# A fused chunk attention and two-layer network on one core: the last two blocks' first layer by 7 products, copies of q shared with GpSimd

## The chip, the cores and the metric

The kernel runs on one core of one Trainium2 chip. A core has a matrix engine, TensorE (PE in the profile, its weight loads PEld), and VectorE (DVE), ScalarE (ACT), GpSimd (POOL) and SyncE (SP), which run in parallel, each through its own list of instructions in order; they wait for each other by semaphores. DMA queues move data between the chip's memory, the on-chip SBUF and back; PE writes its sums to PSUM, from which ACT and DVE read. The metric is the device time of one launch in microseconds (us); lower is better.

## The reference

```python
scores = scale * np.matmul(q_c, k_c.transpose(0, 1, 2, 4, 3))   # chunks of 64 of 576 rows
scores = scores - np.max(scores, axis=-1, keepdims=True)
attn = np.exp(scores)
attn = attn / (np.sum(attn, axis=-1, keepdims=True) + 1e-09)
out = np.matmul(attn, v_c)
...
x = np.ascontiguousarray(attn_out.transpose(0, 2, 1, 3)).reshape(B * S, H * D)
...
h = x @ w_in                       # 4608 x 512 by 512 x 2048
g = np.maximum(0.01 * h, h)
return (g @ w_out).astype(np.float32)   # by 2048 x 512
```

q, k and v are float32 of shape 8 x 8 x 576 x 64: batch, heads, rows, head dimension. Attention stays within chunks of 64 rows. Its output, 4608 tokens by 512, goes through two layers with a leaky ReLU between.

## The kernel before

**Attention** works on 36 tiles of 128 tokens (u, two chunks each, all 8 heads). For a tile, q and k are loaded into a buffer `qk_in` (`NIN` = 9 of them) by DMAs that POOL issues, and turned: for tiles 0 to 9 by PE, from tile 10 by a transposing DMA that SP issues, into a buffer `QKT` (`NKT` = 6). Two copies, one for each half of the partitions, spread q into a zero-padded tile `QZ` (`spread_q`, L506; three tiles in turn). PE multiplies (`Sp`), DVE takes the maximum and subtracts it (`mx`, `sh`), ACT exponentiates (`ex`), DVE sums (`z`), POOL adds the 1e-9 (`ze`), DVE inverts (`zi`), POOL normalises (`en`; DVE for tiles below 9). The result is turned (`et`), PE multiplies by V (`xp`, from two buffers `VB` that hold one batch each, loaded by POOL's DMAs), and ACT stores the tile into `xT`, a ring of 12 tiles.

**The layers** work on 13 blocks of tokens: four of 128, two of 256, seven of 512. Blocks from 4 on do the second layer as a 2 x 2 block product by 7 products instead of 8 (Strassen's scheme): DVE forms four sums of quarters (`form`, L820: `S` and a reused part of `gT`), PE does products 1 to 7 (`product`, L842), each summing into one of three PSUM banks a, b, c, ACT copies intermediate states of bank b to SBUF (`td`, `tu`, `tw`), and DVE adds these to what the other banks hold (`osb`). Bank b carries products 1, 6, 7, 4 one after another, so each must wait until the sum so far has been copied.

**The first layer** of a block is 16 columns of 128 features. Done plainly (`mm1`, L748) a column takes 4 matmuls of 512 tokens (or the same work in two halves of 256, which `SUBS` sets), and ACT applies the ReLU (`gT<-hT`). In blocks 7 to 12 some of it is also done by 7 products: a pair k takes the columns 2k, 2k+1, 8+2k, 9+2k, which are 4 plain columns, and does them as 7 products of 4 matmuls with 256 columns each (`product1`, L953; rows `la`, `lb`, `lc`, named after the bank). `L1S` says which pairs of a block go this way; k = 0 to 3 would be all of it. The products need sums of quarters of x (`xf`, DVE, per block) and of w_in (`wq`, DVE, once per pair). In the trace, a pair's chain on bank b is: product 1, ACT's copy `ld`, product 6, copy `lu`, product 7, copy `lw`, product 4; DVE adds `ld`, `lw` and `lu` to the banks of products 2, 5 and 3; ACT then applies the ReLU to four results. The buffers of `ld`, `lu`, `lw` hold one pair (`temp1`, L970), so a pair's copies wait until the pair ahead of it is done with them; in the last two blocks `ld` has two buffers.

**The order** of every engine is set when the program is built, by a planner (`Planner`): it knows each task's duration from a table in the code, its dependencies and a position (`pos`), and at each step gives an engine the ready task with the lowest position. Positions of attention tasks follow from how far a tile runs ahead of its block (`LEAD`) and from tables of small corrections (`TWEAK`, `NUDGE`, `HOLD`); `LOADS` is the order of the first loads by hand (`g8`: q and k of tile 8; `v1.0`, `v1.1`: the halves of V of batch 1). The hardware runs each engine's list in that order, whatever the real durations are. Where PE has nothing in the first 24 us, filler matmuls (`idle`, L1183) are put.

The lines that set what runs where:

```python
L1S = {7: (0, 1), 8: (0, 1), 9: (0, 2), 10: (0, 1, 2), 11: (1, 2), 12: (0, 1, 2)}
COPY_P = ("ACT",)
ORDER1 = (1, 2, 6, 5, 7, 4, 3)
```

Of the kernel before, what the change touches and what calls it, by code (L numbers as in the profile page):

```python
# [164 lines left out]
def kernel(  # L165
# [31 lines left out]
    SUBS = {11: 512, 12: 512, 10: 512}  # L197
# [11 lines left out]
    ATT = -0.39  # L209
    FORM = -0.93  # L210
    WFAT = -2.31
# [5 lines left out]
    NORM_P = ()  # L217
    EXP8 = ()
    HOLD = {('v', 3): 28.7, ('k', 2): 14.1, ('q', 5, 0): 31.9, ('G', 0, 2, 0): 23.3, ('n', 0): 11.9, ('k', 3): 18.8, ('c', 0): 15.1, ('e', 0): 13.3, ('s', 2): 15.0, ('G', 2, 2, 0): 33.8, ('q', 5, 1): 29.5, ('m', 1): 11.9, ('G', 2, 3, 0): 32.8, ('tq', 0): 6.1, ('tk', 5): 30.8, ('G', 2, 0, 0): 28.6, ('m', 4): 29.4, ('tq', 2): 13.8, ('G', 1, 0, 0): 23.2, ('z', 3): 26.9, ('k', 4): 27.2, ('q', 2, 0): 14.8, ('m', 0): 9.0, ('s', 1): 12.0, ('G', 0, 1, 0): 25.4, ('x', 3): 25.7}
    NUDGE = {('M', 11, 7, 1): -0.03, ('M', 9, 1, 0): 0.01, ('xf', 7, 3): -0.05, ('cm', 10, 2): -0.08, ('L', 12, 1, 2): 0.15, ('form', 7, 3): -0.25, ('A', 11, 15, 0): 0.2, ('L', 12, 0, 1): -0.02}  # L220
    GUARD = 0.84
    DEPTH = 4
    DEEP = 40
    LATE = {'q': 0, 'c': 0, 's': 0.19}
    SPREAD = 1.01
# [4 lines left out]
    MARGIN = 2.08  # L230
    TWEAK = {(0, 4): -0.39, (5, 4): -0.05, (32, 1): 0.26, (4, 11): -0.13, (4, 2): 0.05, (0, 9): 0.13, (2, 2): 1.1, (1, 8): 0.02, (1, 6): 0.3, (9, 7): -0.15, (0, 5): -0.67, (4, 3): 0.2, (26, 9): 0.23, (20, 0): -0.51, (0, 10): -0.12}
    A_LEAD = 0.25
# [354 lines left out]
    def total(u):  # L587
        def emit(eng, tag, at):
            st["z", u] = sbp.tile([128, 8], FP32, name="z", tag="z", bufs=2)
            nc.vector.tensor_reduce(out=st["z", u], in_=st["ex", u], axis=AXL.X, op=ALU.add)  # L590
        return emit
# [83 lines left out]
    for u in range(NU):  # L675
# [35 lines left out]
        if u in ZE:  # L711
            add(("zr", u), dve, total(u), [("x", u)] + prev, pos=p(u, 8))
# [4 lines left out]
        ne = {"DVE": (0.70, 0.74), "POOL": (1.43, 1.48)}  # L717
# [116 lines left out]

    SF_FORMS = (5, 6, 7, 3)
# [4 lines left out]
    ADDED = {2: "d", 5: "w", 3: "u"}  # L840

    def product(j, m, p):  # L842
        def emit(eng, tag, at):
            g, n = gT(j), half_tokens(j)
            bank = BANKS[m]
# [5 lines left out]
            opens = m in OPENS  # L851
# [27 lines left out]
    def finish(j, m, step, p=None):  # L879


        def emit(eng, tag, at):
            ix = slice(None) if p is None else p
            of = BANK[j, BANKS[m]] if p is None else BANK[j, BANKS[m], p]
# [4 lines left out]
            if step == 0:  # L889
                either(eng, to, of)  # L890
            else:
                two = j in TWO2 and m != 3
                by = (BANK[j, "b"] if p is None else BANK[j, "b", p]) if two else temp(ADDED[m], j)[:, ix]
                nc.vector.tensor_tensor(out=to, in0=of, in1=by, op=ALU.add)
# [19 lines left out]
    WQ_: dict[tuple, bass.AP] = {}  # L914
    LB: dict[tuple, bass.AP] = {}
# [13 lines left out]
    def w_form(k, m):  # L929
        def emit(eng, tag, at):  # L930
# [6 lines left out]
            WQ_[k, m] = sbp.tile([128, 2, 256], FP16, name="wq", tag="wq", bufs=4 * len(early))  # L937
# [279 lines left out]
```

## Time and profile before

| | |
|---|---|
| median of 3 runs | 278.14 us (277.4 to 278.62) |
| the profiled execution, its own time | 278.49 us |
| its span, first to last instruction | 276.7 us |
| granted TensorE clock | 1.00 |

The page gives the busy time of each engine over the span. Times of instructions count from the span's start. A row of a timeline has the start, the length of the merged piece, engine, line, operation, what is written and read, and the count; in brackets stands the idle time of the engine just before it and what ended it. Matmuls overlap: a row's length holds the draining of its last matmul, so what a matmul costs PE is the distance from its start to the next one's. The lines that matter are shown where the prediction uses them.

### The profile page before, as it was taken

How to read it: one execution, taken by the hardware profiler on the slowest of the kernel's cores; microseconds unless marked ns; L12 is line 12 of the kernel's file. 1: busy time of each engine (PE TensorE's matmuls, PEld its weight loads, DVE VectorE, ACT ScalarE, POOL GpSimd, SP SyncE). 2: the span in 40 equal slices, each digit the busy share in tenths (PEclk: the TensorE clock that was granted, in tenths of full speed). 3: DMA queues.
4: the chain of work that ended last, by engine and by line, in shares of the span. 5: the costliest groups of instructions: out<-in, count | busy, mean ns of one | idle time of the engine just before them, and what ended most of it. 6: DMA issues, size and time to landing. Idle time of an engine off the chain costs nothing.

```text
span 276.7 us, 7303 instructions
## 1 busy us (share of the span) xinstructions
PE 268.9 (97%) x2992; PEld 231.8 (84%) x2992; DVE 200.0 (72%) x345; ACT 207.3 (75%) x380; POOL 135.4 (49%) x170
## 2 busy tenths in 40 slices
PE   7899999999999999999999999999999999999995
PEld 6789974689999999899999989997887787788884
DVE  7698867886694498679786976797769773854651
ACT  5447764687869898998879889977999478767611
POOL 8857653467774978377576844585220330000000
PEclk9999999999999999999999999999999999999999
DMA  8999999999999999999999999999956103200133
GB/s 141 155 184 161 184 194 155 214 135 182 130 197 165 158 163 191 118 83 145 232 138 152 182 209 165 121 112 242 127 97 172 21 19 97 76 2 0 39 134 133
DMA packets 161152, 38.21 MB, mean 138 GB/s; under 512 B 152160, under 2 KB 156768, under 8 KB 161120
## 3 DMA queue, kind: packets, MB, share of 16 engines
q0 software_dynamic: 114336, 18.09, 97.3%
q1 hardware_dynamic: 45744, 19.41, 38.6%
q8 instruction: 23, 0.38, 0.6%
q10 hardware_dynamic: 1040, 0.26, 0.4%
q14 instruction: 9, 0.07, 0.1%
HBM read 36.70 MB, written 9.44 MB: 167 GB/s over the span
## 4 chain that ended last, share of the span: by engine, by line
PE 82%; DMA 12%; POOL 4%; issue 1%; DVE 0%; POOLq 0%
PE hT L757 23%; PE mb L858 20%; PE mc L858 10%; PE lb L964 9%; PE ma L858 5%; PE lc L964 4%; DMA qk_in<-in_q_dram 4%; DMA w_outT<-in_moe_w_out_dram 4%; DMA qk_in<-in_k_dram 4%; PE xp L648 3%; PE Sp L540 2%; PE la L964 2%; POOL qk_in L327 2%; PE oP L780 2%; POOL w_inT L344 1%; POOL VB L335 1%
## 5 line engine op out<-in xcount | busy, mean ns | idle before, releaser
L757 PE MATMUL hT<-xT,w_inT 128*128 128x256 f16 (+2 forms) x768 | 88.3, 264 | 0.5 <-DMA w_inT<-in_moe_w_in_dram 0.2
L757 PEld LDWEIGHTS <-w_inT 128*128 128x128 f16 x768 | 63.6, 98 | 10.4 <-issue 0.9
L769 ACT ACTIVATE gT<-hT 128x512 f16<-128x512 f32 x88 | 50.6, 593 | 17.0 <-PE hT L757 16.7
L858 PEld LDWEIGHTS <-gT 128*128 128x128 f16 x512 | 49.4, 98 | 6.4
L596 POOL TENSOR_SCALAR ze<-z 128x8 f32<-128x8 f32 x31 | 10.5, 337 | 61.2 <-DVE z L590 60.8
L858 PEld LDWEIGHTS <-S 128*128 128x128 f16 x384 | 36.7, 98 | 4.3
L614 POOL TENSOR_TENSOR en<-ex,zi 128x512 f16<-128x512 f16 x27 | 31.1, 1151 | 15.3 <-ACT xT L658 3.8
L327 POOL DMA_DIRECT2D qk_in<-in_q_dram x39 | 34.1, 875 | 6.2 <-DMA w_outT<-in_moe_w_out_dram 2.6
L327 POOL DMA_DIRECT2D qk_in<-in_k_dram x39 | 34.1, 875 | 4.1 <-DMA w_outT<-in_moe_w_out_dram 1.3
L590 DVE TENSOR_REDUCE z<-ex 128x8 f32<-128x512 f16 x36 | 24.6, 682 | 12.2 <-ACT ex L584 11.8
L549 DVE TENSOR_REDUCE mx<-Sp 128x8 f32<-128x512 f32 x36 | 24.6, 682 | 11.8 <-PE Sp L540 11.6
L858 PE MATMUL mb<-WF,gT 128*128 128x256 f16 x256 | 33.0, 273 | 0.0
L858 PE MATMUL mc<-w_outT,S 128*128 128x256 f16 x256 | 33.0, 273 | 0.0
L276 ACT ACTIVATE QZ<-QKT 64x512 f16<-64x512 f16 x52 | 32.4, 624 | 0.6
L555 DVE TENSOR_TENSOR sh<-Sp,mx 128x512 f32<-128x512 f32 x36 | 24.7, 686 | 0.5
L964 PEld LDWEIGHTS <-wq 128*128 128x128 f16 x224 | 21.5, 98 | 3.3
L658 ACT ACTIVATE xT<-xp 128x512 f16<-128x512 f32 x36 | 21.3, 593 | 3.8 <-PE xp L648 3.6
L584 ACT ACTIVATE ex<-sh 128x512 f16<-128x512 f32 x36 | 22.6, 628 | 1.2 <-DVE sh L555 0.8
L335 POOL DMA_DIRECT2D VB<-in_v_dram x16 | 18.8, 1178 | 3.7 <-DMA w_outT<-in_moe_w_out_dram 1.8
L964 PEld LDWEIGHTS <-w_inT 128*128 128x128 f16 x168 | 16.0, 98 | 2.4
L858 PE MATMUL mb<-WF,S 128*128 128x256 f16 x128 | 16.6, 273 | 0.0
L858 PE MATMUL ma<-w_outT,gT 128*128 128x256 f16 x128 | 16.6, 273 | 0.0
(81 smaller groups left out, 445.1 us busy)
## 6 DMA issues: line engine op xcount, KB each, us to landing
out_dram<-osb SPq DMA_DIRECT2D x12, 512.0 KB, 4.7
VB<-in_v_dram POOLq DMA_DIRECT2D x16, 288.0 KB, 8.0
qk_in<-in_q_dram POOLq DMA_DIRECT2D x31, 128.0 KB, 7.0
qk_in<-in_k_dram POOLq DMA_DIRECT2D x31, 128.0 KB, 7.2
out_dram<-osb SPq DMA_DIRECT2D x10, 256.0 KB, 5.3
w_inT<-in_moe_w_in_dram POOLq DMA_DIRECT2D x8, 256.0 KB, 7.4
w_outT<-in_moe_w_out_dram POOLq DMA_DIRECT2D x4, 512.0 KB, 11.4
qk_in<-in_q_dram POOLq DMA_DIRECT2D x8, 64.0 KB, 7.7
```

The costliest lines, as they stand in the source:

```text
L276: nc.scalar.activation(out=out, in_=in_, func=AFT.Copy, bias=0.0, scale=1.0)
L327: nc.gpsimd.dma_start(out=qk[name, u][a - u * G:z - u * G], in_=SRC[name][a // S, :, a % S:a % S + z - a, :].rearrange("h p d -> p h d"),)
L335: nc.gpsimd.dma_start(out=VB[b % NVB][m * CH:(m + 1) * CH, :, c0:c1, m * CH:(m + 1) * CH], in_=v[b, m * H // 2:(m + 1) * H // 2, c0 * CH:c ...
L549: nc.vector.tensor_reduce(out=st["mx", u], in_=st["S", u], axis=AXL.X, op=ALU.max)
L555: nc.vector.tensor_tensor(out=st["sh", u], in0=st["S", u], in1=st["mx", u].unsqueeze(2).to_broadcast((128, 8, CH)), op=ALU.subtract,)
L584: nc.scalar.activation(out=st["ex", u], in_=st["sh", u], func=AFT.Exp, bias=0.0, scale=SCL)
L590: nc.vector.tensor_reduce(out=st["z", u], in_=st["ex", u], axis=AXL.X, op=ALU.add)
L614: (nc.vector if eng == "DVE" else nc.gpsimd).tensor_tensor(out=st["en", u], in0=st["ex", u], in1=st["zi", u].unsqueeze(2).to_broadcast((12 ...
L757: nc.tensor.matmul(out=hT[:, i, :], lhsT=w_inT[:, t, fc * 128:(fc + 1) * 128], rhs=xT[:, r0 % RING // G:(r0 % RING + tb) // G, t, :], star ...
L769: nc.scalar.activation(out=gT(j)[:, nf * a:nf * a + nf, h * tb:h * tb + tb], in_=HT.pop((j, a, h)), func=AFT.Prelu, bias=0.0, scale=1.0, a ...
L858: nc.tensor.matmul(out=to, lhsT=lhs[:, fc, p * 128:(p + 1) * 128], rhs=rhs[:, fc, :], start=(opens and (p == 0 or j == LAST) and fc == 0), ...
L964: nc.tensor.matmul(out=to[:, i, :], lhsT=lhs[:, t, i * 128:(i + 1) * 128], rhs=rhs[:, :, t, :], start=(m in OPENS and i == 0 and t == 0), ...
```

## The change

The pairs by 7 products become 0, 1, 2 in block 9 and 0 to 3, all of the first layer, in blocks 11 and 12; the pair that stays plain in block 10 is done in halves of 256 tokens. In the last two blocks the copies `ld`, `lu`, `lw` no longer have buffers of their own, but use `qk_in` buffers that the last tiles have left, so that three pairs can be under way at once; the four weight sums of the new pair 3 stand in `QKT` buffers. A pair's last two products change places (`ORDER1`). The copies of q from tile 10 on may run on POOL as well as ACT, and tile 4's normalisation moves from DVE to POOL. In block 10 product 4 of the second layer gets a bank of its own (`SOLO`, rows `me`), and DVE adds it to product 7's copy, where ACT copied the sum before. The order of the first loads, durations of the planner's table (POOL's normalisation 1.16 instead of 1.43, the forms' factor `FSLOW` 1.04 instead of 1.15) and the positions are set anew. Unused variants (`TWO1`, `TWO2`) are removed.

```diff
-    SUBS = {11: 512, 12: 512, 10: 512}
+    SUBS = {12: 512}
...
-    L1S = {7: (0, 1), 8: (0, 1), 9: (0, 2), 10: (0, 1, 2), 11: (1, 2), 12: (0, 1, 2)}
+    L1S = {7: (0, 1), 8: (0, 1), 9: (0, 1, 2), 10: (0, 1, 2), 11: (0, 1, 2, 3), 12: (0, 1, 2, 3)}
...
-    LEAD = 3.86
-    LOADS = 'Q0 i g1 v0.0 g2 v0.1 Q2 g3 Q1 g4 g5 Q3 P2 P0 g7 P1 P3 g6 v1.0 g8 v1.1'
+    LEAD = 4.45
+    LOADS = 'Q0 i g1 v0.0 g2 v0.1 Q2 g3 Q1 g4 g5 Q3 P2 P0 g7 P1 P3 g6 g8 v1.1 v1.0'
...
-    COPY_P = ("ACT",)
+    COPY_P = ("POOL", "ACT")
...
-    NORM_P = ()
+    NORM_P = (4,)
...
-    GUARD = 0.84
+    GUARD = 0
...
-    MARGIN = 2.08
+    MARGIN = 1.79
...
-    ORDER1 = (1, 2, 6, 5, 7, 4, 3)
-    TWO1 = ()
-    TWO2 = ()
-    TWOC = 0.0
-    FSLOW = 1.15
+    ORDER1 = (1, 2, 6, 5, 7, 3, 4)
+    SOLO = (10,)
+    FSLOW = 1.04
...
-        ne = {"DVE": (0.70, 0.74), "POOL": (1.43, 1.48)}
+        ne = {"DVE": (0.70, 0.74), "POOL": (1.16, 1.22)}
...
+    def bank_of(j, m):
+        return "e" if m == 4 and j in SOLO else BANKS[m]
...
-            WQ_[k, m] = sbp.tile([128, 2, 256], FP16, name="wq", tag="wq", bufs=4 * len(early))
+            if early[k] < LAST - 1:
+                WQ_[k, m] = sbp.tile([128, 2, 256], FP16, name="wq", tag="wq", bufs=4 * sum(j < LAST - 1 for j in early.values()))
+            else:
+
+                pair = m in (4, 5)
+                if (k, pair) not in WP_:
+                    WP_[k, pair] = sbp.tile([128, 2, 2, 256], FP16, name="wq", tag="QKT", bufs=NKT)
+                WQ_[k, m] = WP_[k, pair][:, m % 2]
...
-            LT[name, j, k] = sbp.tile(
-                [128, 2, 256], FP32, name=f"l{name}", tag={"d": "sh" if j >= LAST - 1 else "ld", "u": "lw", "w": "lt"}[name],
-                bufs=2 if name == "d" and j >= LAST - 1 else 1,
-            )
+            if j < LAST - 1:
+                tag, bufs = {"d": "ld", "u": "lw", "w": "lt"}[name], 1
+            else:
+                tag, bufs = "qk_in", NIN
+            LT[name, j, k] = sbp.tile([128, 2, 256], FP32, name=f"l{name}", tag=tag, bufs=bufs)
...
+            if j >= LAST - 1:
+
+                n = sum(len(L1S.get(x, ())) for x in range(LAST - 1, j)) + L1S[j].index(k)
+                d_free, u_free, w_free = (
+                    gone("q", min(NU - 1, NU - NIN + 3 * n + 2)) + ([("lg",) + p3 + (m,)] if n > 2 else []) for m in (2, 3, 5)
+                )
...
+            for m, by, deps in ((2, 1, ob0), (5, 7, ob1), (3, 6, ob0)) + (((4, 7, ob1),) if alone else ()):
+                add(nm("cm", m, p), {"DVE": (t_dve, t_dve + 0.03)}, finish(j, m, 1, p), M(m) + [nm("ev", by, p)] + deps, pos=at[m] - 0.2)
```

What this does to the lists of instructions is shown at three places. PE's list is the same up to 45 us of the trace of before. Shortly ahead of that, POOL's list of loads changes. The rows are a piece of the difference; the first two rows are the q and k loads of tile 6, `VB_64` is the V buffer of batch 1, `en` is tile 4's normalisation, and the last q and k row that is common to both is tile 8's before and tile 9's now.

```order
 L327 DMA qk_in<-in_q_dram 128x8x64
 L327 DMA qk_in<-in_k_dram 128x8x64
-L335 DMA VB_64<-in_v_dram 64x36x64
+L327 DMA qk_in<-in_q_dram 128x8x64
+L614 TENSOR_TENSOR en<-ex,zi 128x512
+L327 DMA qk_in<-in_k_dram 128x8x64
+L335 DMA VB_64<-in_v_dram 64x36x64 x2
+L596 TENSOR_SCALAR ze<-z 128x8
 L327 DMA qk_in<-in_q_dram 128x8x64
 L327 DMA qk_in<-in_k_dram 128x8x64
-L335 DMA VB_64<-in_v_dram 64x36x64
```

Tile 8's q load now stands ahead of both V loads, and its k load behind a normalisation.

The second place is POOL's list around the loads of batch 4's V (`VB_63`), near 105 us of the trace of before; first the rows of before.

```order
L614 TENSOR_TENSOR en<-ex,zi 128x512
L327 DMA qk_in<-in_q_dram 64x8x64
L335 DMA VB_63<-in_v_dram 64x36x64 x2
L596 TENSOR_SCALAR ze<-z 128x8
L327 DMA qk_in<-in_k_dram 64x8x64
L614 TENSOR_TENSOR en<-ex,zi 128x512
```

The same place now; the `QZ` rows are copies of q for the scores of tiles 16, 18 and 19.

```order
L280 COPY QZ_67<-QKT 64x8x64 x2
L327 DMA qk_in<-in_k_dram 128x8x64
L596 TENSOR_SCALAR ze<-z 128x8
L335 DMA VB_63<-in_v_dram 64x36x64
L614 TENSOR_TENSOR en<-ex,zi 128x512
L335 DMA VB_63<-in_v_dram 64x36x64
L327 DMA qk_in<-in_q_dram 64x8x64
L280 COPY QZ_66<-QKT 64x8x64 x2
L327 DMA qk_in<-in_q_dram 64x8x64
L596 TENSOR_SCALAR ze<-z 128x8
L280 COPY QZ_67<-QKT 64x8x64
L614 TENSOR_TENSOR en<-ex,zi 128x512
```

Five copies of q, which stood on ACT, now stand between the loads and the normalisations. In all, 25 of the 52 copies of q from tile 10 on moved to POOL.

The third place is ACT's list while block 12's first layer runs; first the rows of before, where the pairs follow one another with plain columns (`gT<-hT`) between them.

```order
L769 ACTIVATE gT<-hT 128x512
L276 ACTIVATE ld<-lb 128x512
L992 ACTIVATE gT<-lu 128x2x256
L276 ACTIVATE lu<-lb 128x512
L276 ACTIVATE tu<-mb 128x512
L276 ACTIVATE lw<-lb 128x512
L992 ACTIVATE gT<-ld 128x2x256
L992 ACTIVATE gT<-lb 128x2x256
L992 ACTIVATE gT<-lw 128x2x256
```

Now three pairs run side by side, and their copies stand one behind the other.

```order
L276 ACTIVATE ld<-lb 128x512
L276 ACTIVATE tu<-mb 128x512
L1003 ACTIVATE gT<-ld 128x2x256
L276 ACTIVATE lu<-lb 128x512 x3
L276 ACTIVATE lw<-lb 128x512 x2
L1003 ACTIVATE gT<-lw 128x2x256
L1003 ACTIVATE gT<-lb 128x2x256
L1003 ACTIVATE gT<-lw 128x2x256
L1003 ACTIVATE gT<-lu 128x2x256
```

The plain columns are gone, and PE's list has at this place the second products of three pairs in a row (12 matmuls `lb<-xf,wq`) and right behind them the third product of the first pair.

More of the change, by code (lines that the diff above doesn't have):

```diff
@@ L711 @@
         if u in ZE:
-            add(("zr", u), dve, total(u), [("x", u)] + prev, pos=p(u, 8))
+            add(("zr", u), {e: {"DVE": (0.69, 0.72), "POOL": (TOTALC, TOTALC + 0.06)}[e] for e in (TOTAL if u >= 9 else ("DVE",))}, total(u), [("x", u)] + prev, pos=p(u, 8))
             add(("ze", u), {"POOL": (0.25, 0.30)}, guard(u), [("zr", u)], pos=p(u, 8))
@@ L844, in emit @@
             g, n = gT(j), half_tokens(j)
-            bank = BANKS[m]
+            bank = bank_of(j, m)
             lhs, rhs = {
@@ L891, in emit @@
             else:
-                two = j in TWO2 and m != 3
-                by = (BANK[j, "b"] if p is None else BANK[j, "b", p]) if two else temp(ADDED[m], j)[:, ix]
-                nc.vector.tensor_tensor(out=to, in0=of, in1=by, op=ALU.add)
+                nc.vector.tensor_tensor(out=to, in0=of, in1=temp(ADDED[m], j)[:, ix], op=ALU.add)
         return emit
```

83 lines of the change are left out of this document (37 added, 46 removed).

## The prediction

> **What bounds the kernel now.** The page comes first, for the share of each engine.
>
> ```profile
> span 276.7 us, 7303 instructions
> PE 268.9 (97%) x2992; PEld 231.8 (84%) x2992; DVE 200.0 (72%) x345; ACT 207.3 (75%) x380; POOL 135.4 (49%) x170
> ```
>
> PE is busy 97% of the span, but that is an average; the view by stretches of time says where the other 3% lies (columns: length of the stretch, then busy us of PE, PEld, DVE, ACT and POOL, the granted clock, DMA share, GB/s).
>
> ```profile
> 50.00:205.00 155.00, 155.00 (x1711) 137.27 (x1710) 117.35 (x196) 133.95 (x247) 97.13 (x117) 1.00 1.79 161
> 205.00:235.00 30.00, 30.00 (x299) 24.05 (x297) 20.00 (x32) 22.88 (x42) 5.93 (x8) 1.00 0.28 71
> 235.00:260.00 25.00, 25.00 (x216) 20.86 (x215) 14.94 (x22) 17.88 (x33) 0.00 (x0) 1.00 0.06 23
> 260.00:277.00 17.00, 13.37 (x123) 11.74 (x120) 7.87 (x12) 3.79 (x9) 0.00 (x0) 1.00 0.34 124
> ```
>
> From 50 to 260 us PE has no idle time at all, at full clock. A PE that never waits can be made shorter in two ways only: fewer matmul slots, or less waiting before 50 us. It can be made longer by any wait that the new order puts into those 210 us. So the sum has three terms: slots saved, a start-up wait saved, waits added.
>
> **The slots saved.** A busy matmul overlaps the next one, so its price is the distance of starts, read from the timeline (start, length, line, tile, count).
>
> ```profile
> 227.38 0.60 PE L964 MATMUL la<-xT,w_inT 128*128 128x256 f16 x4
> 227.82 1.04 PE L964 MATMUL lb<-xf,wq 128*128 128x256 f16 x8
> 228.69 0.60 PE L964 MATMUL lc<-xf,wq 128*128 128x256 f16 x4
> 229.13 1.03 PE L757 MATMUL hT<-xT,w_inT 128*128 128x512 f16 x4
> 229.99 0.40 PE L648 MATMUL xp<-et,VB 128*128 128x64 f16 x8
> ```
>
> Four matmuls of a product take 227.82 - 227.38 = 0.44 us (227.38 to 229.13 is 1.75 for 16, so 0.109 each), four plain matmuls of 512 columns 229.99 - 229.13 = 0.86 (0.216 each). A pair done plainly is 16 of these, 3.46 us; done by 7 products it is 28 of the narrow ones, 3.06 us: 0.40 saved per pair. The pairs done by products go from 14 to 18 (block 9 from two to three, 11 from two to four, 12 from three to four).
>
> ```profile
> L757 PE MATMUL hT<-xT,w_inT 128*128 128x512 f16 x64 | 16.1, 379 | 0.0
> ```
>
> All 64 wide matmuls go: -64 x 0.216 = -13.82 us. 112 narrow product matmuls come: +112 x 0.109 = +12.23. The plain 256-column matmuls stay 448 (32 fewer in block 9, 32 more in block 10, whose remaining pair is now cut in halves). **Term one: -1.59 us.** It is a count of the built instruction streams, so I do not doubt it; the other PE work, the filler matmuls of the start and the last 17 us of PE's order are the same in both.
>
> **The start-up wait.** The first three rows are POOL's issues, then one of DVE and three of PE; the last three are issue-to-landing times of the first V load, the q load and the second V load.
>
> ```profile
> 32.96 1.15 POOL L335 DMA_DIRECT2D VB<-in_v_dram  x1 [1.82 <-DMA w_outT<-in_moe_w_out_dram]
> 35.50 0.88 POOL L327 DMA_DIRECT2D qk_in<-in_q_dram  x1 [1.39 <-DMA w_outT<-in_moe_w_out_dram]
> 37.68 1.15 POOL L335 DMA_DIRECT2D VB<-in_v_dram  x1 [0.42 <-issue]
> 39.43 0.20 DVE L602 RECIPROCAL zi<-ze 128x8 f32<-128x8 f32 x1
> 46.40 1.03 PE L780 MATMUL oP<-w_outT,gT 128*128 128x512 f16 x4
> 47.73 0.40 PE L502 MATMUL qp<-ident,qk_in 128*128 128x128 f16 x4 [0.30 <-DMA qk_in<-in_q_dram]
> 51.01 0.40 PE L648 MATMUL xp<-et,VB 128*128 128x64 f16 x8
> ...
> DMA to landing us min/median/max: 13.6/13.6/13.6
> DMA to landing us min/median/max: 12.2/12.2/12.2
> DMA to landing us min/median/max: 12.9/12.9/12.9
> ```
>
> The transpose of tile 8's q could have started at 46.40 + 0.86 = 47.26 and started at 47.73, when its load (35.50 + 12.2) had landed: 0.47 us lost. The queue served V (landed 32.96 + 13.6 = 46.56), then 128 KB of q 1.1 us later, so V's 288 KB cost about 2.5 us (an estimate from those two landings). With V behind tile 8's loads, q lands near 45.2 and the wait is gone. The new bound stands right behind it: PE then reaches its first use of the new V at 51.01 - 0.47 = 50.54, while both V loads together land no earlier than before, 37.68 + 12.9 = 50.58. A normalisation now stands ahead of the k load on POOL; it can start when tile 4's sums are inverted (the row of DVE, 39.4), so k is issued near 41 with 4 us of older transfers still queued, and nothing runs dry. **Term two: -0.43 us** (between -0.47 and 0, the last if V comes late).
>
> **What is added beside PE.** The groups that price it (busy us, mean ns of one):
>
> ```profile
> L614 POOL TENSOR_TENSOR en<-ex,zi 128x512 f16<-128x512 f16 x27 | 31.1, 1151 | 15.3 <-ACT xT L658 3.8 <-ACT gT L769 3.6 <-DVE zi L602 2.2
> L596 POOL TENSOR_SCALAR ze<-z 128x8 f32<-128x8 f32 x31 | 10.5, 337 | 61.2 <-DVE z L590 60.8
> L276 ACT ACTIVATE QZ<-QKT 64x512 f16<-64x512 f16 x52 | 32.4, 624 | 0.6
> L987 DVE TENSOR_TENSOR ld<-la,ld 128x512 f32<-128x512 f32 x14 | 9.6, 688 | 7.0 <-PE la L964 4.3 <-ACT ld L276 2.6
> L276 ACT ACTIVATE ld<-lb 128x512 f32<-128x512 f32 x14 | 8.3, 594 | 3.1 <-PE lb L964 3.0
> ```
>
> ACT loses 25 of its 52 q copies (-25 x 0.62 = -15.6 us) and 16 activations of the wide sums (-16 x 0.6 = -9.6); four pairs bring 28 copies and activations (+28 x 0.6 = +16.8). Net about -8. DVE gets 12 additions (12 x 0.69 = 8.3), the four sums of the fourth pair's weights (at most 0.7 each) and block 10's addition (0.7), and loses one normalisation: +11 at most, spread over stretches where it is busy 60 to 75%. All of this is hidden as long as PE's order never reaches a product early.
>
> POOL gets 25 copies of 64x512, an operation that no row shows. Bounds: 0.34 us (the 128x8 guard) and 1.15 (the normalisation, which reads two tiles of that length). I take 0.7, nearest the normalisation: two data streams instead of three, 2/3 of its undisturbed 1.04 below. That is +17.5 us on POOL, up to +29, and not below +8. The Trainium skill, GPSIMD Engine Reference, section 3.1, states 769 ns for a tight loop over 512 elements, and its section on engine selection that one-input operations run roughly at line rate; by that figure the copies would add 19 us (an estimate) and the sum for PE would be the same. No row of this case shows it.
>
> One cost of the neighbourhood is in the trace: POOL's normalisation and DVE's forms of four quarters hold each other up.
>
> ```profile
> 118.20 1.04 POOL L614 TENSOR_TENSOR en<-ex,zi 128x512 f16<-128x512 f16 x1 [0.41 <-DVE zi L602]
> ...
> 154.50 1.90 POOL L614 TENSOR_TENSOR en<-ex,zi 128x512 f16<-128x512 f16 x1 [1.20 <-ACT osb L276]
> ...
> 154.28 1.23 DVE L831 TENSOR_TENSOR S<-S,gT 128x2048 f16<-128x2048 f16 x1
> 155.42 2.06 DVE L831 TENSOR_TENSOR gT<-gT 128x2048 f16<-128x2048 f16 x1
> ```
>
> The normalisation began inside the first form and took 1.90 instead of 1.04; the next form then took 2.06 instead of 1.23: about 0.85 us each way. Yet PE lost nothing to it in this stretch, so the order had room. The Trainium skill, SBUF — State Buffer, "Who interferes with whom", speaks against this change: a VectorE instruction with two SBUF inputs and a GpSimd one that reads SBUF exclude each other, and the later one blocks. These rows agree (1.90 and 2.06); by that rule each of the 25 copies is a new chance for such a block.
>
> Where would it show? A tile's scores wait for both copies of its q. The tightest place now is tile 19:
>
> ```profile
> 116.70 0.63 ACT L276 ACTIVATE QZ<-QKT 64x512 f16<-64x512 f16 x1
> ...
> 117.54 0.40 PE L540 MATMUL Sp<-QKT,QZ 128*128 128x64 f16 x8
> ```
>
> The copy ends at 117.33, PE starts 0.2 us later. A copy of 0.7 instead of 0.62 fits; one that is blocked for 0.85 does not. And POOL works in order: behind a blocked copy stand the next normalisation, the guard that DVE's inverse waits for, and the q, k and V loads.
>
> The last stretch has the tightest chain. Within a pair, each sum of the shared bank must be copied by ACT before the next product adds to it:
>
> ```profile
> 242.22 0.60 PE L964 MATMUL lb<-xf,wq 128*128 128x256 f16 x4
> ...
> 242.86 0.60 ACT L276 ACTIVATE lw<-lb 128x512 f32<-128x512 f32 x1 [1.09 <-PE lb L964]
> 244.17 0.60 ACT L992 ACTIVATE gT<-lb 128x512 f16<-128x512 f32 x1 [0.71 <-PE lb L964]
> 244.66 0.62 ACT L992 ACTIVATE gT<-ld 128x512 f16<-128x512 f32 x1
> ...
> 243.53 0.60 PE L964 MATMUL lb<-xT,wq 128*128 128x256 f16 x4
> ```
>
> From one product to the next of its chain: 243.53 - 242.22 = 1.31 us, with PE not waiting. In the new order of block 12 the second products of three pairs stand one after the other and the first pair's third right behind: 3 x 0.437 = 1.31 us. No margin is left, and ACT must be free on time; just ahead of it stands an activation that waits for DVE. ACT starts one instruction every 0.5 us there (244.17 to 244.66); from the three copies to the first product of block 12's second layer PE has 21 products and 4 second-layer pieces, 21 x 0.437 + 4 x 0.874 = 12.7 us, and ACT 21 instructions, 10.5 to 12.8 us by spacing or by length. It fits, closely.
>
> **Term three, waits added: +0.3 us**, between 0 (the order of before has none in 210 us) and 3.5 (below); I take the value near the lower end: one blocked copy beyond its room or one missed slot of that chain. Sum: -1.59 - 0.43 + 0.3 = -1.72. The profiled execution took 278.49 us with a span of 276.7 (1.8 outside it) and would become 276.8 with a span of 275.0; it lies 0.35 above the median of the runs shown, 278.14, so the forecast is **276.4**.
>
> **The rivals.** A measurement of this kernel can tell about 0.5% from no change: 276.75 and 279.53 are the borders.
> - *Forecast, waits up to 0.6 us*: 276.1 to 276.75. For it: no PE wait in the rows from 50 to 260 although ACT was fuller than it will be. Chance 0.54.
> - *Blocked copies take the gain back.* Three of the shortest distances between copy and scores are overrun by 0.85 - 0.4 each, 1.3 us: 278.14 - 2.02 + 1.3 = 277.4. By the SBUF page's rule this is what more POOL work brings. Against it: the blocks quoted above cost PE nothing. Chance 0.20.
> - *The three pairs make ACT or DVE the bound at the end.* Each of the three chains misses one slot by 0.3 and the last form is late by as much: 1.2 us, 277.3. Chance 0.14.
> - *POOL's queue becomes the bound, slower than before.* Its fullest stretch:
>
> ```profile
> 100.00:112.00 12.00, 12.00 (x148) 10.90 (x145) 10.29 (x19) 10.70 (x20) 9.16 (x11) 1.00 2.00 178
> ...
> qk_in<-in_q_dram POOLq DMA_DIRECT2D x31, 128.0 KB, 7.0
> ```
>
> POOL is busy 9.2 of 12 us; five copies come there (tiles 16, 18, 19). At 0.7 it is 12.7, and the order can push loads behind; at 1.15 each it is 14.9, 2.9 over, and with one block of 0.85 less 0.2 of room PE waits 3.5 us: 278.14 - 2.02 + 3.5 = 279.6. It decides from a copy of about 1 us on. Against it: a load takes 7.0 us from issue to landing (the second row), so one issued a little later finds the queue still full. Chance 0.12.
>
> The range takes in all but the last case and some luck: 275.9 (no added wait, and 0.2 for the spread of runs) to 278.6. Faster by over 0.5%: 0.54; within: 0.20 + 0.14 = 0.34; slower: 0.12.
>
> **What would show it.** Term one: no 128x512 row of hT, and 288 matmuls with wq instead of 224. Term two: no idle time ahead of the q transposes near 47 us, the first use of the second V buffer near 50.6. Term three: the stretches from 50 to 255 us full on PE; if not, the releaser named ahead of Sp (a POOL copy) or of lb (ACT) says which rival it is. POOL copies near 0.7 us are right; near 1.1 the fourth case is on. The forecast is wrong if PE shows more than 0.6 us of idle time there.

## The result, and the profile after

| | before | after |
|---|---|---|
| median (runs) | 278.94 us (22: 277.4 to 280.4) | 277.23 us (22: 276.27 to 279.38) |
| the profiled execution, its own time | 278.49 us | 277.59 us |
| its span | 276.7 us | 275.8 us |

The ratio of the times is 0.994, 95% interval 0.992 to 0.996: the change is faster by 1.1 to 2.2 us. The forecast was 276.4 from a median of 278.14, that is 1.72 less; over more runs the kernel before stands at 278.94, and the change is 1.71 below it. A second set of 12 runs of the change, further down, gave 0.9983 (0.995 to 1.0015; such a ratio is not the quotient of the two medians), so the size is known less well than the first interval says. Three runs more than 1.5% above the fastest of their kernel, one of the kernel before and two of one variant, are left out of the ratios but not of the medians. The traces are sharper than the times, and the account below is made with them.

The page's head of the changed kernel:

```profile
span 275.8 us, 7478 instructions
PE 268.1 (97%) x3040; PEld 236.7 (86%) x3040; DVE 208.2 (76%) x362; ACT 198.4 (72%) x365; POOL 151.1 (55%) x196
```

ACT went from 207.3 to 198.4 us busy, POOL from 135.4 to 151.1, DVE from 200.0 to 208.2. PE has 48 matmuls more and still ends sooner, since the new ones are narrower. The view by stretches, for the stretches that the prediction showed (columns as there):

```profile
50.00:205.00 155.00, 154.61 (x1723) 137.96 (x1722) 120.93 (x205) 123.13 (x228) 112.21 (x141) 1.00 1.87 161
205.00:235.00 30.00, 30.00 (x318) 27.02 (x316) 24.07 (x38) 24.57 (x46) 5.90 (x10) 1.00 0.22 66
235.00:260.00 25.00, 25.00 (x237) 22.39 (x236) 17.00 (x25) 18.52 (x36) 0.00 (x0) 1.00 0.08 29
100.00:112.00 12.00, 12.00 (x138) 10.86 (x137) 11.46 (x20) 7.86 (x15) 9.28 (x13) 1.00 1.90 182
```

PE is full from 205 to 260 us, where three pairs now run side by side. It lost 0.39 us between 50 and 205, where before it lost none. POOL between 100 and 112 is no fuller than before (9.28 against 9.16), where the prediction's fourth case had counted 12.7 us of work.

**How much of the gain lies where.** Up to some 45 us every execution waits for its first loads, and by a different amount each time. So each trace is read from tile 10's scores on: from their start to the start of the last matmul. The rows are tile 10's scores and the last piece of PE's order; the last of a piece's eight matmuls starts 7 x 0.109 = 0.76 us behind the piece's start. First the timeline of the kernel before:

```profile
69.03 0.40 PE L540 MATMUL Sp<-QKT,QZ 128*128 128x64 f16 x8
...
272.33 1.04 PE L858 MATMUL mc<-w_outT,S 128*128 128x256 f16 x8
```

The same two places after:

```profile
69.06 0.40 PE L540 MATMUL Sp<-QKT,QZ 128*128 128x64 f16 x8
...
271.43 1.04 PE L861 MATMUL mc<-w_outT,S 128*128 128x256 f16 x8
```

Before it is 204.07 us, after 203.13: 0.94 less. I call it the **steady part** from here on. It repeats well: the second profiled execution of the change gave 203.15, although its tile 10 came at 70.29 instead of 69.06. Over the twelve traces of this study, those of the variants included, tile 10's scores start between 67.6 and 71.5 us, a range wider than that of the 22 times of either kernel.

**The two waits of the steady part.** The timeline near tile 20 (start, length, engine, line, operation, tiles, count, idle time and its releaser):

```profile
111.44 1.91 PE L757 MATMUL hT<-xT,w_inT 128*128 128x256 f16 x16
111.71 1.05 POOL L614 TENSOR_TENSOR en<-ex,zi 128x512 f16<-128x512 f16 x1
111.80 1.80 DVE L929 TENSOR_TENSOR xf<-xf,xT 128x512 f16<-128x512 f16 x1
...
112.70 1.38 POOL L280 COPY QZ<-QKT 64x512 f16<-64x512 f16 x2
...
113.52 0.83 DVE L929 TENSOR_TENSOR xf<-xT 128x512 f16<-128x512 f16 x1
...
113.65 0.60 PE L973 MATMUL lb<-xf,wq 128*128 128x256 f16 x4 [0.30 <-DVE xf L929]
```

The 16 plain matmuls are worth 16 x 0.109 = 1.75 us, so the product could have started at 113.19; it started at 113.65: 0.46 lost (the row's 0.30 counts from the modelled end of the matmul ahead). It waited for a sum of quarters that took 1.80 us. The sum began 0.09 behind POOL's normalisation, and two copies of q stand right behind that: it ended only after the normalisation and the first copy were through (112.70 + 0.61 = 113.31, and the sum's end is 113.60). The group says what such a sum takes otherwise (min/median/max ns):

```profile
L929 DVE TENSOR_TENSOR xf<-xf,xT x6: 410/417/1803, 111.8 to 242.4; 128x512 f16<-128x512 f16 x6
```

The other wait is near 165 us:

```profile
163.37 1.04 POOL L614 TENSOR_TENSOR en<-ex,zi 128x512 f16<-128x512 f16 x1 [0.38 <-issue]
163.70 0.99 DVE L929 TENSOR_TENSOR xf<-xT 128x512 f16<-128x512 f16 x1
...
164.62 0.68 DVE L555 TENSOR_TENSOR sh<-Sp,mx 128x512 f32<-128x512 f32 x1
164.77 0.60 PE L973 MATMUL lb<-xf,wq 128*128 128x256 f16 x4
...
165.36 0.30 PEld L540 LDWEIGHTS <-QZ 128*128 128x128 f16 x8 [0.27 <-POOL QZ L280]
165.39 0.39 PE L540 MATMUL Sp<-QKT,QZ 128*128 128x64 f16 x8
```

The scores could have started at 164.77 + 0.44 = 165.21 and lost 0.18. The row names a copy of q, but that had ended at 165.16; 0.07 ahead of the scores' weight load, at 165.36, DVE's `sh` ends (164.62 + 0.68), which has to read the scores' PSUM bank empty before the next tile's scores may go there. In all nine traces with this wait, two of them without any copy of q on POOL, PE's weight load starts 0.06 to 0.08 us behind the end of that `sh`. `sh` was late because a sum ahead of it took 0.99: it ended 0.28 behind a normalisation, and the copy right behind that one, at 164.36, was the one held here (0.80 instead of 0.61). 0.46 + 0.18 = 0.64 is the whole of the waits, and -1.59 + 0.64 = -0.95 is the measured -0.94.

**The start.** The rows of PE around the q transposes of tile 8 and the first use of the new V:

```profile
46.67 1.03 PE L780 MATMUL oP<-w_outT,gT 128*128 128x512 f16 x4
47.53 0.39 PE L502 MATMUL qp<-ident,qk_in 128*128 128x128 f16 x4
...
50.80 0.63 PE L648 MATMUL xp<-et,VB 128*128 128x64 f16 x8
51.27 0.60 PE L780 MATMUL oP<-w_outT,gT 128*128 128x512 f16 x2
```

The q transposes start 0.86 us behind the four wide matmuls ahead of them: no wait is left there. V is a little late instead. The eight matmuls of `xp` are worth 8 x 0.029 = 0.23 us, and the next work started 0.47 behind their start: 0.24 lost, inside the piece. So this stretch gained 0.47 and gave 0.24 back in this execution. Tile 10's scores start no sooner for it (69.06 against 69.03), because the changed kernel already stood 0.27 later at 45 us, behind the same matmuls. In the other ten traces with the new order of loads the wait at tile 8's q is gone too; the wait at V is 0.42, 0.67 and 0.77 in three of them, whose rows name the V load, and absent in seven. So V took back between nothing and more than the 0.47, and what the new loads are worth in time can't be seen behind a start that moves by more than that.

**POOL's copies.** Min/median/max of the copies of q on POOL, in ns:

```profile
L280 POOL COPY QZ<-QKT x25: 599/609/884, 69.6 to 208.1; 64x512 f16<-64x512 f16 x25
```

### The profile page after: what moved, and what is told of

The parts are those of the page before. It is cut to its first block, busy times and chain, and to the rows that moved or that the text cites. A ratio compares the mean times of both kernels' runs of the same rounds, so it can differ in the third digit from the quotient of the medians.

```text
span 275.8 us, 7478 instructions
## 1 busy us (share of the span) xinstructions
PE 268.1 (97%) x3040; PEld 236.7 (86%) x3040; DVE 208.2 (76%) x362; ACT 198.4 (72%) x365; POOL 151.1 (55%) x196
## 4 chain that ended last, share of the span: by engine, by line
PE 80%; DMA 8%; POOL 6%; DVE 3%; issue 1%; ACT 1%; POOLq 0%
PE mb L861 19%; PE hT L757 16%; PE lb L973 11%; PE mc L861 10%; PE lc L973 6%; PE ma L861 5%; DMA w_outT<-in_moe_w_out_dram 4%; PE oP L780 4%; DMA qk_in<-in_k_dram 4%; PE la L973 3%; PE xp L648 3%; PE Sp L540 2%; POOL qk_in L327 2%; POOL VB L335 2%; POOL w_inT L344 1%
## 5 line engine op out<-in xcount | busy, mean ns | idle before, releaser
L757 PE MATMUL hT<-xT,w_inT 128*128 128x256 f16 (+1 forms) x704 | 71.8, 253 | 0.3 <-DMA w_inT<-in_moe_w_in_dram 0.2
L757 PEld LDWEIGHTS <-w_inT 128*128 128x128 f16 x704 | 57.6, 98 | 5.9 <-issue 0.6
L769 ACT ACTIVATE gT<-hT 128x512 f16<-128x512 f32 x72 | 41.3, 594 | 14.6 <-PE hT L757 14.2
L973 PEld LDWEIGHTS <-wq 128*128 128x128 f16 x288 | 27.9, 98 | 3.8 <-issue 0.5
L861 PE MATMUL mb<-WF,gT 128*128 128x256 f16 x240 | 30.9, 273 | 0.0
L973 PEld LDWEIGHTS <-w_inT 128*128 128x128 f16 x216 | 20.2, 98 | 2.1
L973 PE MATMUL lb<-xf,wq 128*128 128x256 f16 x144 | 21.0, 273 | 0.3 <-DVE xf L929 0.3
L997 DVE TENSOR_TENSOR lw<-lc,lw 128x512 f32<-128x512 f32 x18 | 12.4, 688 | 8.9 <-ACT lw L276 8.8
L280 POOL COPY QZ<-QKT 64x512 f16<-64x512 f16 x25 | 16.2, 647 | 2.5 <-DMA QKT<-qk_in 1.7
```

The source lines that it names most:

```text
L757: nc.tensor.matmul(out=hT[:, i, :], lhsT=w_inT[:, t, fc * 128:(fc + 1) * 128], rhs=xT[:, r0 % RING // G:(r0 % RING + tb) // G, t, :], star ...
L769: nc.scalar.activation(out=gT(j)[:, nf * a:nf * a + nf, h * tb:h * tb + tb], in_=HT.pop((j, a, h)), func=AFT.Prelu, bias=0.0, scale=1.0, a ...
L861: nc.tensor.matmul(out=to, lhsT=lhs[:, fc, p * 128:(p + 1) * 128], rhs=rhs[:, fc, :], start=(opens and (p == 0 or j == LAST) and fc == 0), ...
L973: nc.tensor.matmul(out=to[:, i, :], lhsT=lhs[:, t, i * 128:(i + 1) * 128], rhs=rhs[:, :, t, :], start=(m in OPENS and i == 0 and t == 0), ...
```

## The experiments

All of them are told by three things: the median, the ratio to the kernel before in the same set of runs (95% interval), and the steady part of the profiled execution. "Lost" is worked out as above, by distances of starts.

| | median us (runs) | ratio | steady part us |
|---|---|---|---|
| before | | | 204.07 |
| the change | 277.23 (22) | 0.994 (0.992 to 0.996) | 203.13 |
| the change again | 277.58 (12) | 0.9983 (0.995 to 1.0015) | 203.15 |
| copies of q on ACT | 281.68 (6) | 1.0129 (1.0091 to 1.0167) | 207.36 |
| tile 20's copies on ACT | 278.06 (12) | 0.9986 (0.9963 to 1.0009) | 203.46 |
| pairs as before | 279.51 (12) | 1.0024 (0.9995 to 1.0053) | 204.52 |
| each POOL copy twice | 280.89 (10) | 1.0085 (1.0056 to 1.0115) | 205.49 |
| one set of pair buffers | 281.08 (4) | 1.0115 (1.0057 to 1.0173) | 206.47 |
| before, new order of loads | 279.57 (12) | 1.0037 (1.0013 to 1.0062) | 205.48 |
| tile 20's copies on DVE | 276.44 (10) | 0.9931 (0.9906 to 0.9957) | 202.68 |
| the same again | 278.09 (12) | 0.995 (0.9919 to 0.9982) | 202.67 |
| all POOL copies on DVE | 279.14 (12) | 1.0004 (0.9973 to 1.0035) | 204.27 |

### The change again

No edit.

> The changed kernel once more, beside the variants on one chip. Both theories: ratio to the kernel before 0.994, within 0.003; PE waits after 50 us near 0.65 us in sum, at the product lb behind DVE's xf near 113 us (0.46) and at the scores near 165 us (0.18). If those two waits move about from run to run, they are not a property of the order.

Measured: the two waits are there again, 0.48 and 0.18 us, and the steady part is 203.15. The median is 1.19 below that of the kernel before in the same runs (277.58 against 278.77), but the ratio, 0.9983, is above the 0.997 that was expected at most, and its interval holds 1. What follows: the waits belong to the order, not to one execution; the size of the gain in whole time is not settled better than between 0 and 2 us by the two sets together, but in the steady part it is 0.92 to 0.94.

### Copies of q on ACT

```diff
-            either(eng, QZ[u % NQZ][part, :, :, s, :], src[part])
+            either(eng if u in BY_PE["q"] else "ACT", QZ[u % NQZ][part, :, :, s, :], src[part])
```

The 25 copies of POOL stand at their places on ACT; the rest of the order is that of the change.

> Every copy of q from tile 10 on is issued on ACT at the place in the order where the planner had put it on POOL; nothing else moves. Theory 'lock' (POOL's normalisation and the copies behind it hold up DVE's sums of two SBUF tiles): the xf near 112 us takes at most 1.3 us instead of 1.80, the PE wait behind it falls from 0.46 to under 0.1; ACT carries 25 x 0.62 = 15.5 us more (about 214 us) and has room for it, since it carried 207 before; time 0 to 0.5 us below the changed kernel. Rival 'relief of ACT' (the gain needs the copies off ACT): ACT falls behind an order that was made without them, PE waits over 1 us after 50 us, released by ACT, and the time goes back to within 0.3% of the kernel before.

The steady part grew by 4.2 us, with 14 waits of 0.1 to 0.7. Both theories missed: the time is 1.3% above the kernel before, where the first had it at or below the change's and the rival within 0.3% of before. Its busy times from 50 to 205 us (columns as before):

```profile
50.00:205.00 155.00, 153.32 (x1692) 135.56 (x1691) 115.99 (x200) 134.40 (x246) 97.13 (x117) 1.00 1.71 158
```

And one of the waits, from its timeline:

```profile
210.39 0.63 ACT L276 ACTIVATE QZ<-QKT 64x512 f16<-64x512 f16 x1
...
210.93 0.57 ACT L276 ACTIVATE lu<-lb 128x512 f32<-128x512 f32 x1
...
211.55 0.60 PE L973 MATMUL lb<-xf,wq 128*128 128x256 f16 x4 [0.41 <-ACT lu L276]
```

A copy of q stands ahead of `lu`, and the product behind `lu` comes late. ACT's total is about that of the kernel before over 50 to 205 us (134.4 against 133.95), so it is not its load but its order: chains of pairs that have little margin, with copies in between. The wait at tile 20's sums is there too, 0.44 us, though no copy stands on POOL; under 0.1 was expected:

```profile
112.42 1.47 DVE L929 TENSOR_TENSOR xf<-xf,xT 128x512 f16<-128x512 f16 x1
```

The sum stands beside a normalisation alone (112.54 to 113.60), but it begins only 1.09 us ahead of the time at which its product is due, where the change has 1.39 (111.80 and 113.19). What follows: in this order the saved slots are had only because 25 copies left ACT. The order was planned for POOL; one planned for ACT was not tried.

### Tile 20's copies on ACT

```diff
-            either(eng, QZ[u % NQZ][part, :, :, s, :], src[part])
+            either("ACT" if u == 20 else eng, QZ[u % NQZ][part, :, :, s, :], src[part])
```

> Only tile 20's two copies of q, which stand behind a normalisation on POOL near 112.7 us, are issued on ACT instead. Theory 'lock': the xf near 111.8 us is held by the normalisation alone, about 1.3 instead of 1.80 us, and the PE wait of 0.46 us near 113 falls under 0.1; the wait near 165 us (0.18) stays; span 0.3 to 0.5 us shorter after 110 us. Rival (the xf waits for something else, the buffer of the block ahead or its input): the wait stays over 0.3 us.

The sum, and the wait that came instead:

```profile
110.35 1.26 DVE L929 TENSOR_TENSOR xf<-xf,xT 128x512 f16<-128x512 f16 x1
...
113.21 0.63 ACT L276 ACTIVATE QZ<-QKT 64x512 f16<-64x512 f16 x1
...
113.86 0.60 ACT L276 ACTIVATE lu<-lb 128x512 f32<-128x512 f32 x1
...
114.50 0.60 PE L973 MATMUL lb<-xf,wq 128*128 128x256 f16 x4 [0.62 <-ACT lu L276]
```

The sum took 1.26 instead of 1.80, and the product behind it no longer waits. The next product of the chain lost 0.78 instead, to a copy of q ahead of `lu`; the steady part is 203.46, 0.33 worse. What follows: with tile 20's copies off POOL the wait near 113 us goes, as the theory said; but where they stand on ACT now they cost more than that.

### Pairs as before

```diff
-    SUBS = {12: 512}
+    SUBS = {11: 512, 12: 512, 10: 512}
...
-    L1S = {7: (0, 1), 8: (0, 1), 9: (0, 1, 2), 10: (0, 1, 2), 11: (0, 1, 2, 3), 12: (0, 1, 2, 3)}
+    L1S = {7: (0, 1), 8: (0, 1), 9: (0, 2), 10: (0, 1, 2), 11: (1, 2), 12: (0, 1, 2)}
```

The rest of the change stays, and the order is planned anew.

> The changed kernel with the pairs of before (14 instead of 18, wide columns in the last three blocks), planned anew with the rest of the change. Theory 'slots': PE gets 64 wide matmuls for 112 narrow ones, +1.59 us; with waits as in the change the ratio to the kernel before is 0.998 to 1.002. Rival 'order' (the gain is that of the new positions and of the work shared between engines, not of the products): ratio 0.993 to 0.996, as the change.

The steady part is 204.52. It holds one wait, of 0.48, at tile 20's sums again; without it, 204.04 against 204.07 before. The ratio, 1.0024, is just above the 0.998 to 1.002 of the theory and far from the rival's 0.993 to 0.996. What follows: all other parts of the change, in the order planned with them, bring nothing to the steady part; its gain is the slots of the four pairs.

### Each POOL copy twice

```diff
             either(eng, QZ[u % NQZ][part, :, :, s, :], src[part])
+            if eng == "POOL":
+                either(eng, QZ[u % NQZ][part, :, :, s, :], src[part])
```

> Each of the 25 copies on POOL is done twice over (the second writes the same values again), so a copy costs about 1.25 us instead of 0.65; POOL goes from 151 to about 167 us. It tries the fourth rival of the prediction, POOL's queue as the bound, which was to decide from about 1 us per copy. If that holds: 2 to 4 us of new PE waits, released by POOL's copies or by DVE sums that they hold up, most of them between 95 and 125 us. If the distances between copy and scores (0.6 to 12 us in the changed kernel) are room enough: under 1 us of new waits.

Its timeline at the two largest waits:

```profile
114.01 2.02 DVE L931 TENSOR_TENSOR xf<-xf,xT 128x512 f16<-128x512 f16 x1
...
116.08 0.60 PE L975 MATMUL lb<-xf,wq 128*128 128x256 f16 x4 [1.37 <-DVE xf L931]
...
141.09 1.57 POOL L280 COPY QZ<-QKT 64x512 f16<-64x512 f16 x2
...
142.71 0.29 PEld L542 LDWEIGHTS <-QZ 128*128 128x128 f16 x8 [0.87 <-POOL QZ L280]
```

The steady part grew by 2.36 us: 1.54 lost at tile 20's sums, 0.75 where scores wait for a copy that now takes 1.57 in its two goes (the row of POOL, and PE's weights behind it), 0.27 and less elsewhere. What follows: with two goes, about 1.3 us, in the place of one copy of 0.65, the kernel is slower than the one before the change, and the added 2.36 us lie within the 2 to 4 that were expected. Most of it is not POOL's queue as the bound but DVE's sums that it holds up; scores that wait for POOL itself cost the 0.75.

### One set of pair buffers

```diff
-            if j < LAST - 1:
+            if True:
                 tag, bufs = {"d": "ld", "u": "lw", "w": "lt"}[name], 1
...
-            if j >= LAST - 1:
+            if False:
```

The copies `ld`, `lu`, `lw` of the last two blocks go into the buffers of the earlier blocks, which hold one pair; the pairs stay, and the order is planned anew.

> All of the first layer of the last two blocks by products, but with the one set of buffers for ld, lu, lw that the blocks ahead have, planned anew: a pair's copies wait for the pair ahead. Theory 'three at a time is what lets the last two blocks go wholly by products': a chain step is 1.31 us, a pair's chain near 4 us, and PE runs out of other work in block 12: 1 to 4 us of PE waits after 200 us, released by ACT. Rival (PE has enough other work, the buffers bring nothing): under 0.3 us of new waits.

From its timeline in block 12:

```profile
260.41 0.60 PE L973 MATMUL lb<-xf,wq 128*128 128x256 f16 x4 [0.75 <-ACT lu L276]
...
261.05 0.60 ACT L276 ACTIVATE lw<-lb 128x512 f32<-128x512 f32 x1 [0.41 <-PE lb L973]
...
261.69 0.60 PE L973 MATMUL lb<-xT,wq 128*128 128x256 f16 x4 [0.69 <-ACT lw L276]
```

The last pair's chain stands bare: PE waits for ACT's copy, ACT for PE's product, in turn. Five waits between 259 and 265 us lose 3.25 us; the steady part is 206.47, 3.34 longer. What follows: with one pair at a time the new pairs cost more than their slots save. Three at a time hides the chain; two at a time were not tried.

### The kernel before with the new order of loads

```diff
-    LOADS = 'Q0 i g1 v0.0 g2 v0.1 Q2 g3 Q1 g4 g5 Q3 P2 P0 g7 P1 P3 g6 v1.0 g8 v1.1'
+    LOADS = 'Q0 i g1 v0.0 g2 v0.1 Q2 g3 Q1 g4 g5 Q3 P2 P0 g7 P1 P3 g6 g8 v1.1 v1.0'
```

The order of the kernel before is planned anew with it.

> The kernel before with tile 8's loads ahead of both loads of batch 1's V and nothing else edited (planned anew). Theory: the wait of 0.47 us ahead of tile 8's q transpose near 47 us is gone; behind it PE waits 0 to 0.25 us for V near 51 us, so 0.2 to 0.45 us are won, which is 0.1 to 0.2% and lies inside the spread of the start; from tile 10's scores on as before (204.07 us, up to what the new plan changes). Rival: the wait only changes its place (V), nothing is won by tile 9's scores.

Its timeline at tile 8, and at the largest wait of its steady part:

```profile
47.30 1.03 PE L780 MATMUL oP<-w_outT,gT 128*128 128x512 f16 x4
...
48.16 0.39 PE L502 MATMUL qp<-ident,qk_in 128*128 128x128 f16 x4
...
195.82 1.03 PE L858 MATMUL mb<-WF,gT 128*128 128x256 f16 x8 [0.69 <-ACT tw L276]
```

The wait for tile 8's q is gone (48.16 - 47.30 = 0.86). But the planner, given the new loads, put the rest into another order, with 0.85, 0.38 and 0.23 us lost at three places after 190 us, far from any load. The steady part is 205.48, and the kernel is slower by 0.1 to 0.6%. What follows: the part of the mechanism that was predicted is there; its gain of 0.46 was less than what a re-planned order can lose elsewhere, so this run doesn't measure it alone. A run that changes the loads and keeps every other list as it was was not made.

### Tile 20's copies on DVE, and the same again

```diff
-            either(eng, QZ[u % NQZ][part, :, :, s, :], src[part])
+            either("DVE" if u == 20 else eng, QZ[u % NQZ][part, :, :, s, :], src[part])
```

> Tile 20's two copies of q go to DVE, at their place in the order, which is behind the two xf sums there; ACT's list is that of the change. Theory 'lock, and ACT has no room there': the xf near 112 us is held by the normalisation alone (1.26 instead of 1.80 us), PE's wait near 113 us falls from 0.46 to under 0.1, and no new wait of the chain behind it (0.78 with ACT) appears; from tile 10's scores to the last matmul 202.6 to 202.8 us instead of 203.14. Rival (the sums wait for something else than POOL's lock): 203.0 or more.

The timeline at tile 20's sums:

```profile
111.50 1.91 PE L757 MATMUL hT<-xT,w_inT 128*128 128x256 f16 x16
...
111.78 1.06 POOL L614 TENSOR_TENSOR en<-ex,zi 128x512 f16<-128x512 f16 x1
111.86 1.27 DVE L929 TENSOR_TENSOR xf<-xf,xT 128x512 f16<-128x512 f16 x1
...
113.05 0.41 DVE L929 TENSOR_TENSOR xf<-xT 128x512 f16<-128x512 f16 x1
...
113.25 0.60 PE L973 MATMUL lb<-xf,wq 128*128 128x256 f16 x4
...
113.38 0.28 DVE L278 COPY QZ<-QKT 64x512 f16<-64x512 f16 x1
```

The sum took 1.27 and the next one 0.41 instead of 0.83; the product starts on time (111.50 + 1.75 = 113.25). The steady part is 202.68: 0.45 less than the change's, the wait that went. The copies, 0.28 each behind the sums, cost nothing.

> The same kernel as the run with tile 20's two copies on VectorE, once more. If its gain over the change comes from the one wait near 113 us (0.46 us), 202.65 to 202.7 us from tile 10's scores to the last matmul again (the change: 203.13 and 203.15), one wait of 0.18 near 165, and a time of 276.2 to 277.2, ratio 0.990 to 0.995. If the order of such a wait moves from run to run, it would come back or another appear, at 203.1 us or more.

202.67 again, with the 0.18 wait near 167 us (all of it later by 2.3, as tile 10 was). The whole time, 278.09, missed the 276.2 to 277.2 that was expected; the ratio is at the upper end. What follows: in this order the wait near 113 us came from two copies of q standing behind a normalisation on POOL, and moving them to DVE takes it away. The normalisation still holds the sum, which now ends just in time: at 111.86 + 1.27 = 113.13 in the rows above, for a product due at 113.25. This is the best kernel of the study by its steady part; by whole time it beats the kernel before in both sets, and the change itself by less than these runs can tell.

### All POOL copies on DVE

```diff
-            either(eng, QZ[u % NQZ][part, :, :, s, :], src[part])
+            either("DVE" if eng == "POOL" else eng, QZ[u % NQZ][part, :, :, s, :], src[part])
```

> The 25 copies of q that the change puts on GpSimd stand at the same places on VectorE instead; all else is the change. A copy took 0.28 us on VectorE where tile 20's stood there, and 0.65 on GpSimd. Theory one (what matters is that ScalarE and TensorE's order are relieved; GpSimd costs something by locking VectorE's sums): VectorE has room for 25 x 0.28 = 7 us, the 0.46 us wait near 113 us stays gone, and from tile 10's scores to the last matmul it is 202.6 to 203.2 us, against 203.13 in the change; time 276.0 to 277.2, ratio to before about 0.990 to 0.995. Rival (VectorE stands as near the order's due times as ScalarE, where the same copies cost 4.2 us): new waits of TensorE for VectorE's forms, sums or shifts of scores, 1 to 4 us in all; 204.1 to 207 us from tile 10's scores to the last matmul, time 278 to 281, ratio 0.998 to 1.010.

The group of the copies (count, busy us, mean ns):

```profile
L278 DVE COPY QZ<-QKT 64x512 f16<-64x512 f16 x25 | 9.2, 369 | 1.3 <-DMA QKT<-qk_in 0.9
```

The timeline at the largest wait:

```profile
112.32 1.91 PE L757 MATMUL hT<-xT,w_inT 128*128 128x256 f16 x16
...
113.24 1.47 DVE L929 TENSOR_TENSOR xf<-xf,xT 128x512 f16<-128x512 f16 x1
113.36 1.06 POOL L614 TENSOR_TENSOR en<-ex,zi 128x512 f16<-128x512 f16 x1
...
114.76 0.60 PE L973 MATMUL lb<-xf,wq 128*128 128x256 f16 x4 [0.53 <-DVE xf L929]
```

The steady part is 204.27, 1.14 worse than the change's: five waits of 0.70, 0.58, 0.26, 0.16 and 0.08. The rival had the sign and the lower end of its size; the first theory is wrong. The sum is reached later: 0.83 us ahead of the time at which its product is due (113.24, against 112.32 + 1.75 = 114.07 behind the plain matmuls), where the change has 1.39 (111.80 and 113.19). A normalisation alone is then enough to make it late. What follows: one tile's two copies fit on DVE, all 25 do not in this order; some copies have to stand on POOL.

## Why the prediction was right, and where it was off

- **What bounds the kernel**: right. Every gain and loss of the steady part, in all twelve traces, is a number of matmul slots or a wait of PE.
- **Term one, slots, -1.59 us**: right. The steady part less its waits went from 204.07 to 203.13 - 0.64 = 202.49, which is -1.58; with the pairs alone put back it is 204.04.
- **Term two, the start, -0.43**: right in mechanism, too large in size. The wait for tile 8's q went (0.47), and V became the next bound as the prediction said, but it cost 0.24 rather than 0.04, with V's second load landing at 51.0 instead of 50.58: -0.23 in the profiled execution. Nor was 0 the worst that V could make of the term: with the same loads it cost 0.67 and 0.77 in two other traces. In the second execution the wait at tile 8 and that at V both were absent, and three others, 1.75 us together, stood ahead of them between 30 and 43 us; the start as a whole is not known to better than that.
- **Term three, waits, +0.3**: its size was off, 0.64 instead of 0.3 by distances of starts (0.39 by the busy time of PE, where 0.6 was to mark the forecast as wrong), and its mechanism was another one. The prediction looked at the copies of q as the ones held up, and at the scores behind them. It was the sums `xf` on DVE that were held up by POOL, once through a normalisation and a copy of q (1.80 instead of 0.42), once by a normalisation alone (0.99). The copies themselves had a median of 0.61 and a maximum of 0.88. The rule of the Trainium skill, SBUF — State Buffer, "Who interferes with whom", named the right mechanism, that VectorE and GpSimd exclude each other and the later one blocks. The traces agree with the exclusion, and less well with who blocks: in the run with all copies on DVE the sum began, by the trace, 0.12 us ahead of the normalisation (113.24 and 113.36), and it was still the sum that was held, until 0.29 behind the normalisation's end. The step that failed was to apply the mechanism to the newcomer alone and not to everything on DVE that stands beside it.
- **The sum**: the three terms as measured give -1.59 - 0.23 + 0.64 = -1.18. The profiled executions differ by -0.90 (278.49 and 277.59), because the change stood 0.27 later before any of the three; the medians differ by -1.71 and -1.19 in the two sets. Terms two and three were each off by 0.2 to 0.35 to the same side; the forecast of -1.72 matched the first medians to 0.01, and that closeness is luck. The time itself, 276.4, is 0.83 below the measured 277.23, because it stood on three runs with a median of 278.14, which is 0.80 below that of 22.
- **A copy on POOL, 0.7 us**: measured 0.65 mean. The figure of the Trainium skill, GPSIMD Engine Reference, section 3.1, was 769 ns for a tight loop over 512 elements; this copy, on 64 partitions of 512 elements in 16 bits, is 0.61 at the median.
- **The last stretch**: right. The chain of three pairs held with no margin. The rows are those of block 12:

```profile
244.32 1.94 PE L973 MATMUL lb<-xf,wq 128*128 128x256 f16 x16
245.02 1.57 ACT L276 ACTIVATE lu<-lb 128x512 f32<-128x512 f32 x3 [0.69 <-PE lb L973]
```

  The first third product starts behind 12 matmuls at 244.32 + 1.31 = 245.63, and the first `lu` is through by about then; PE went on without a gap. With one pair at a time the same chain cost 3.34 us.
- **The rivals**: no scores waited for a blocked copy; what blocking cost, 0.64 of the 1.3 that it was given, it cost through sums on DVE. Three pairs did not make ACT or DVE the bound. POOL's queue did not become the bound. With each copy done twice the time was 280.89, where 279.6 was forecast for that case, but only 0.75 of the 2.36 us added came by its path, scores that wait for a copy.

## What to carry to other kernels

Where TensorE never waits, count matmul slots first; that number came out to 0.01 us, and the rest of a change is whether the other engines can hold the new order. When an instruction is moved to GpSimd, ask which VectorE instruction stands beside it and who waits for that one, not only whether the moved one is late. A new plan of the order moves waits of half a microsecond to places that have nothing to do with the edit, so measure an edit with the order held, or read the trace for the waits it brought.

## What the runs showed of the hardware

- At tile 20 a VectorE sum that took 0.42 us elsewhere was held until a GpSimd normalisation beside it was through, and ended 0.29 behind it: 1.27 where it began 0.08 behind the normalisation, 1.47 where it began 0.12 ahead of it. With two GpSimd copies right behind the normalisation it was held over the first of them too, 1.80. The normalisation itself kept its 1.05.
- It is not always so: near 164 us of the change another sum ended 0.28 behind its normalisation although a copy stood right behind that, and the copy took 0.80 instead of 0.61. What decides which of the two goes first, these runs don't show.
- The same copy of 64 x 512 in 16 bits took 0.28 us on VectorE at tile 20 (0.37 mean of 25), 0.61 on GpSimd and 0.62 on ScalarE.
- The steady part after the start repeated to 0.02 us between two executions, for each of two kernels, while their starts moved by 1.2 and 2.4 us. So two profiles can tell a few tenths of a microsecond, where the interval of 12 runs of the change was 1.8 us wide.
